# Keeping the second parts of w2 in DRAM, splitting the scores of all heads, and decoding weights in three Vector pieces

## The chip, the cores and the metric

The kernel runs on one core of a Trainium2 chip. The metric is the time of one execution on the device in microseconds (us). Five engines work beside each other and each takes its instructions strictly in the order in which the program issues them: TensorE (PE in the profile; its weight loads stand apart as PEld), VectorE (DVE), ScalarE (ACT), GpSimd (POOL) and SyncE (SP), which here issues all DMAs.

## The reference

Causal attention with a per-token decay, over 8 batches of 8 heads, 576 tokens, head size 64; then a layer norm and an MLP with a residual over the 4608 tokens of width 512 that the heads make.

```python
scores = q @ k.T / 8                                   # per head, 576 x 576
cum    = cumsum(log(clip(f, 1e-4, 1)))                 # per head
scores = where(causal, -1e9, scores + cum[:, None] - cum[None, :])
attn   = softmax(scores)                               # with 1e-9 in the denominator
x      = attn @ v                                      # heads side by side: 4608 x 512
xn     = (x - mean(x)) / sqrt(var(x) + 1e-6) * g_ln
out    = x + relu(xn @ w_ch1) @ w_ch2                  # 512 -> 2048 -> 512
```

w_ch1 and w_ch2 arrive as float64; q, k, v, f and the result are float32.

## The kernel before, in words

**Precision.** TensorE takes float32 at a slower rate and a rounded kind, float32r, at a faster one. The kernel gets float32 accuracy from the faster kind by splitting an operand into two parts, the rounded value ("high") and what is left ("low" or second part), and adding the products of high with high, high with low, and low with high. The MLP does this for weights and activations: `w1h`, `w1l`, `w2h`, `w2l` hold all parts of both weights in SBUF. Of the 64 heads (n = 8 x batch + head) the first 16 (`NFULL`) are done with plain float32 matmuls for scores and for the output; they are called full. The others split q, k, v and the probabilities.

**Weights (`WPrep`).** There are 32 items, w1 and w2 in turn, each 128 x 512 float64 values. An item is loaded as 512 KB of raw words (`wr`, 3 buffers), scaled by ScalarE (line 160, tile `wy`), decoded from float64 to float32 by four pieces on VectorE (lines 176, 177, 180, 172), the last followed by a sum on GpSimd (line 173); a w1 item also gets a column sum on TensorE (`colsum`, line 191) and four pieces that centre it (`centre`, line 199). Then ScalarE writes the high part (line 215) and GpSimd the second part (line 219). One call of `tick` moves this pipeline on by one item; the VectorE pieces go into a queue, and `fill` issues a few of them at a time. `ready()` is the number of ticks made less 5; `done()` says that all ticks (37) are made and the queue is empty.

**Slots.** The program is written as a list of 256 slots, four per head (t = 1 to 4, one tile of 128 query rows each; t = 1 also has the first 64 rows), and three slots to drain. What a slot issues, and in which order, is a string of letters; the last entry whose first slot is reached holds:

```python
ORDERS = [
    (0, "WwQsSthAeMrgFBmlLNPaRf"),
    (37, "WwQSstAMhPelgLNFrfmBRa"),
    (66, "AthQFlMSPNreamLRB"),
]
...
            elif c == "W":
                due = 1 + min(u, W_CHANGE) / W_SLOTS + max(0, u - W_CHANGE) * W_TICKS
                while not wp.done() and wp.tick_no <= due:
                    wp.tick()
```

Q: score matmuls of slot u (lines 357 to 360). S: mask, row maximum and move to SBUF on VectorE (383). e: exponential with row sum on ScalarE (394). B: reciprocal of the sum on VectorE (399, 400) and scaling on GpSimd (401). t, h, l: two slots later (`LAG`) the probabilities are transposed on TensorE (407), copied by ScalarE (457), and, for heads that are not full, their second parts made by VectorE (462). A: three slots later the output matmuls (470 or 492), for two tiles together. F, a: the output goes to `xs` (523, or 526 and 537) and for two heads together to DRAM. P: `prep`, which loads and splits the next heads (lines 329 to 344). w, g, f: `fill` with 1, 2 or 3 pieces. s: column sums. W: ticks, as above, u being the slot.

**The MLP (`Moe`)** works on chunks of 256 tokens, 18 in all, each in 16 steps j over 128 columns of the hidden layer. A step is `mm1` (12 matmuls, lines 569 to 571), a Relu and its second part (577, 582), and, one slot later, `mm2` (6 matmuls, lines 591 to 593). Letters M, r, m are the step's first half, N is `second()`, which does `mm2` of the step before, R is `rest()`, which loads and splits the next chunk's input. A slot issues its step only if `moe.can(wp.ready())` was true at its start and u is 35 or more. `can` asks that the weights of step j are there (ready at least 2(j + 1)) and that the chunk's input is. Steps left after the slots run in a loop of their own behind them.

At head 14, t = 1 (slot 56), `prep` makes all ticks that are left, closes the pool of the weight pipeline's tiles and opens the pool `late`, which holds the tiles of the split heads.

Of the kernel before, what the change touches and what calls it, by code (L numbers as in the profile page):

```python
# [11 lines left out]
I32 = mybir.dt.int32  # L12
U16 = mybir.dt.uint16
AF = mybir.ActivationFunctionType
# [4 lines left out]
P = 128  # L19
# [17 lines left out]
W_ASIDE = 6  # L37
FILL = {"f": 3, "g": 2, "w": 1}
# [17 lines left out]
def attn_moe(ctx: ExitStack, tc: tile.TileContext, qk, v, f, g, w1, w2, out):  # L56
# [6 lines left out]

    early = ExitStack()
    wpool = early.enter_context(tc.tile_pool(name="early", bufs=1))
    pools = {}

# [42 lines left out]
    def gates(h0):  # L110
        nc.vector.tensor_scalar(out=fa, in0=fa, scalar1=1e-4, scalar2=1.0, op0=ALU.max, op1=ALU.min)
        nc.scalar.activation(fb, fa, AF.Ln)
        nc.vector.tensor_tensor_scan(out=fc, data0=fones, data1=fb, initial=0.0, op0=ALU.mult, op1=ALU.add)
        nc.scalar.activation(cumr[:, 0, :], fc, AF.Copy, scale=-1.0 / SCALE)
        nc.vector.scalar_tensor_tensor(
            out=cumr[:, 1, :], in0=fc, scalar=-1.0 / SCALE, in1=cumr[:, 0, :].bitcast(F32), op0=ALU.mult, op1=ALU.subtract
        )
        nc.sync.dma_start(out=h0.kl[64:66, :], in_=cumr[0:1].bitcast(F32))
        nc.sync.dma_start(out=cumd, in_=cumr.bitcast(F32))
# [12 lines left out]
    class WPrep:  # L132
# [8 lines left out]
        def load(self, n):  # L141
# [7 lines left out]
            else:  # L149
                nc.sync.dma_start(out=raw, in_=w2.bitcast(U32)[j * P : (j + 1) * P, :])  # L150
            self.d[n] = {"raw": raw, "hw": raw.rearrange("p (n t) -> p n t", t=2)[:, :, 1]}

# [9 lines left out]
        def decode(self, n):  # L162
            layer, j = self.items[n]
            d = self.d[n]
            y, z = d["y"], d["hw"]
            low = d["raw"].bitcast(U16).rearrange("p (n t) -> p n t", t=4)[:, :, 1]
            zf, yf = z.bitcast(F32), y.bitcast(F32)
            d["w"] = yf
            ve = nc.vector

            def last():
                ve.scalar_tensor_tensor(out=zf, in0=low, scalar=2.0**-36, in1=zf, op0=ALU.mult, op1=ALU.mult)
                nc.gpsimd.tensor_tensor(out=yf, in0=yf, in1=zf, op=ALU.add)

            return [
                lambda: ve.tensor_scalar(out=z, in0=z, scalar1=0x80000000, scalar2=None, op0=ALU.bitwise_and),  # L176
                lambda: ve.scalar_tensor_tensor(  # L177
                    out=y, in0=y, scalar=3, in1=z, op0=ALU.logical_shift_left, op1=ALU.bitwise_or
                ),
                lambda: ve.tensor_scalar(out=z, in0=y, scalar1=0xFF800000, scalar2=None, op0=ALU.bitwise_and),  # L180
                last,
            ]
# [22 lines left out]
        def parts(self, n):  # L205
            layer, j = self.items[n]
            w = self.d[n]["w"]
            if layer == 1:
                fs = slice(j * P, j * P + P)
                return w.rearrange("p (k f) -> p k f", k=KT), w1h[:, :, fs], w1l[:, :, fs]  # L210
            return w, w2h[:, j, :], w2l[:, j, :]

        def high(self, n):
            w, hi, lo = self.parts(n)
            nc.scalar.copy(out=hi, in_=w)

        def low(self, n):
            w, hi, lo = self.parts(n)
            nc.gpsimd.tensor_tensor(out=lo, in0=w, in1=hi.bitcast(F32), op=ALU.subtract)
            del self.d[n]  # L220

        def tick(self):
# [19 lines left out]
            if on(t - 2 - cl, 1):  # L242
                self.high(t - 2 - cl)
            if on(t - 3, 2):
                self.low(t - 3)
# [21 lines left out]
        def done(self):  # L267
            return self.tick_no >= len(self.items) + 3 + W_SUMS and not self.queue

# [19 lines left out]

    xqs, xfs = [], []  # L290

    def new_xq(name, dt):
        xq = work.tile([66, S], dt, tag="xq", bufs=2, name=name)
        nc.gpsimd.memset(xq[64:66, :].bitcast(F32), 1.0)
        return xq

    def load(n):
        h = Head()
        h.n, h.full = n, n < NFULL
        if h.full:  # L300
            h.kl = work.tile([66, S], F32, tag="kl", bufs=2, name=f"kl{n}")
            if len(xfs) < 2:
                xfs.append(new_xq(f"xf{n}", F32))
            h.xq = xfs[n % 2]
            nc.sync.dma_start(out=h.xq[0:64, :], in_=qk[n][0:64, 0, :])
            nc.sync.dma_start(out=h.kl[0:64, :], in_=qk[n][0:64, 1, :])
            if n > 0:
                nc.sync.dma_start(out=h.kl[64:66, :], in_=cumd[n])
        else:
            h.raw = pools["late"].tile([P, 2, S], F32, tag="raw", bufs=1, name=f"raw{n}")  # L310
            nc.sync.dma_start(out=h.raw, in_=qk[n])
        return h
# [8 lines left out]
    def prep_a(h):  # L321
        n = h.n
        h.hi = pools["late"].tile([P, 2, S], F32R, tag="hi", bufs=2, name=f"hi{n}")
        h.kl = work.tile([66, S], F32R, tag="kl", bufs=2, name=f"kl{n}")
        if len(xqs) < 2:
            xqs.append(new_xq(f"xq{len(xqs)}", F32R))
        h.xq = xqs[(n - NFULL) % 2]
        nc.sync.dma_start(out=h.kl[64:66, :].bitcast(F32), in_=cumd[n])
        nc.scalar.copy(out=h.hi[:, 1, :], in_=h.raw[:, 1, :])
# [4 lines left out]
    def prep_b(h):  # L334
        nc.scalar.copy(out=h.hi[:, 0, :], in_=h.raw[:, 0, :])  # L335
        nc.vector.tensor_copy(out=h.xq[0:64, :], in_=h.raw[0:64, 0, :])
        nc.gpsimd.tensor_tensor(  # L337
# [10 lines left out]
    def qk_mm(h, t):  # L348
# [4 lines left out]
        for i, (a, z) in enumerate(cuts):  # L353
            sp = bank(f"s{h.n}_{t}_{i}")[:m, : z - a]
            xq, kl = h.xq[:, q0 : q0 + m], h.kl[:, a:z]
            if h.full:
                mm(sp, xq, kl, start=True, stop=True)  # L357
            else:
                mm(sp, h.hi[:, 0, q0 : q0 + m], h.hi[:, 1, a:z], start=True, stop=False)  # L359
                mm(sp, xq, kl, start=False, stop=True)  # L360
            h.s[t].append((a, z, sp))
# [51 lines left out]
    def transpose_unit(h, t):  # L413
# [3 lines left out]
        if t <= 2:  # L417
            if t == 1:
                h.ph1 = work.tile([P, 704], F32 if h.full else F32R, tag="ph1", bufs=1, name=f"ph1_{n}")
                h.pl1 = None if h.full else pools["late"].tile([P, 384], F32R, tag="pl1", bufs=1, name=f"pl1_{n}")  # L420
            ph = h.ph1
# [14 lines left out]
        else:  # L436
            if t == 3:
                h.ph2 = work.tile([P, 9 * P], F32 if h.full else F32R, tag="ph2", bufs=1, name=f"ph2_{n}")
                h.pl2 = None if h.full else pools["late"].tile([P, 7 * P], F32R, tag="pl2", bufs=1, name=f"pl2_{n}")
            c = 0 if t == 3 else P  # L440
# [72 lines left out]
    def finish(h):  # L513
# [10 lines left out]
        else:  # L524
            tmp = pools["late"].tile([P, S1], F32, tag="ot", bufs=1, name=f"ot{h.n}_{c0}")
            nc.scalar.copy(out=tmp[js, :w], in_=po[64:128, :w])
# [58 lines left out]

    def mm2(c, j, h):
        if j == 0:
            c.acc = [ps.tile([P, DM], F32, tag=f"acc{i}", bufs=1, name=f"acc{c.n}_{i}") for i in range(2)]
        for i in range(2):
            ts_ = slice(P * i, P * i + P)  # L590
            mm(c.acc[i], h[:, 0, ts_], w2h[:, j, :], start=(j == 0), stop=False)  # L591
            mm(c.acc[i], h[:, 0, ts_], w2l[:, j, :], start=False, stop=False)  # L592
            mm(c.acc[i], h[:, 1, ts_], w2h[:, j, :], start=False, stop=(j == FT - 1))  # L593
# [60 lines left out]
    class Moe:  # L654
# [3 lines left out]
        def fetch(self):  # L658
# [75 lines left out]
    load_v(hd[0])  # L734
    consts()
    gates(hd[0])
    wp.tick()
    for u, slot in enumerate(slots):
# [12 lines left out]
        def piece(c):  # L751
# [53 lines left out]
        def prep():  # L805

            if slot is not None:
                if t == 1 and n + 1 < NFULL:
                    start_head(n + 1)
# [11 lines left out]
                if t == 3 and n + 2 >= NFULL and n + 2 < B * H:  # L821
                    start_head(n + 2)
# [8 lines left out]
    while moe.left() > 0 or moe.prev is not None:  # L831
# [5 lines left out]
        moe.second()  # L837
        moe.rest()


# [36 lines left out]
```

## Time and profile before

| what | value |
|---|---|
| median of 3 runs | 1269.73 us |
| lowest and highest of them | 1265.62, 1269.95 us |
| profiled execution, its own time | 1260.39 us |
| span of its profile (first to last instruction) | 1258.6 us |
| mean granted TensorE clock | 0.992 |
| moved by DMA | 100.42 MB, mean 80 GB/s |

The page of the profile gives busy time by engine, the span in 40 slices, the chain of work that ended last, and the costliest groups of instructions by line of the program. A group's row reads: line, engine, operation, tile written and tiles read, shapes, count; then busy time in us and the mean length of one in ns; then the engine's idle time just before it and what ended it. A row of windows reads: stretch, its length, then busy time and number of instructions of each engine in the order PE, PEld, DVE, ACT, POOL (only the engines that the chosen lines use), granted clock, DMA share and GB/s.

### The profile page before, as it was taken

What the parts mean: (1) busy time and instruction counts of PE and PEld (TensorE: products, weight loads), DVE (VectorE), ACT (ScalarE), POOL (GpSimd) and SP (SyncE); (2) the same over time, 40 slices, a digit from 0 to 9 for tenths busy, and PEclk for the clock granted to TensorE, in tenths of its full rate; (3) what the DMA queues carried; (4) which work ended last, traced back from release to release, by engine and by line L of the source; (5) the groups of instructions that cost most, each with busy time, mean ns of one, the idle gap of its engine ahead of it and who ended that gap; (6) DMA issues with size and microseconds to landing.
All of it is one profiled execution on the core that took longest, in us unless ns stands there. A gap on an engine that the chain in (4) does not pass through costs nothing.

```text
span 1258.6 us, 24937 instructions
## 1 busy us (share of the span) xinstructions
PE 1232.6 (98%) x8148; PEld 1082.0 (86%) x8148; DVE 844.8 (67%) x2948; ACT 639.1 (51%) x1904; POOL 454.9 (36%) x545
## 2 busy tenths in 40 slices
PE   7999998999999999999999999999999999999998
PEld 5666766789999999999999999999998999999997
DVE  5879999358686868686868777777767773233232
ACT  4776555455555555555656565555555552112111
POOL 4666666243333433334344433333434330000000
PEclk8999989999999999999999999999999999999999
DMA  5444452122322232222222222323232201110100
GB/s 154 130 128 140 134 144 74 64 72 72 92 76 89 79 92 76 79 89 76 79 80 78 69 79 74 92 75 93 76 92 75 87 33 44 44 41 17 51 26 26
DMA packets 91250, 100.42 MB, mean 80 GB/s; under 512 B 26864, under 2 KB 76016, under 8 KB 91120
## 3 DMA queue, kind: packets, MB, share of 16 engines
q1 hardware_dynamic: 91120, 98.82, 25.5%
q8 instruction: 65, 1.06, 0.3%
q14 instruction: 65, 0.53, 0.1%
HBM read 79.61 MB, written 19.17 MB: 78 GB/s over the span
## 4 chain that ended last, share of the span: by engine, by line
PE 86%; DVE 10%; issue 1%; POOL 1%; ACT 1%; DMA 1%; SPq 0%; DVEq 0%; POOLq 0%; ACTq 0%
PE h L570 11%; PE h L569 10%; PE h L571 10%; PE acc L591 10%; PE acc L592 10%; PE acc L593 10%; PE tr L407 7%; PE o L492 5%; PE s L359 3%; PE s L360 3%; PE o L470 3%; DVE wy L177 2%; PE s L357 2%; DVE wr L176 1%; DVE wr L180 1%
## 5 line engine op out<-in xcount | busy, mean ns | idle before, releaser
L401 POOL TENSOR_SCALAR p<-p,st 64x64 f32<-64x64 f32 (+4 forms) x320 | 179.0, 564 | 428.1 <-DVE st L400 146.3
L570 PE MATMUL h<-x,w1h 128*128 128x256 f32 x1152 | 326.6, 283 | 3.0 <-DVE x L554 3.0
L569 PE MATMUL h<-x,w1h 128*128 128x256 f32 x1152 | 329.1, 286 | 0.0
L571 PE MATMUL h<-x,w1l 128*128 128x256 f32 x1152 | 325.2, 282 | 0.0
L577 ACT ACTIVATE hh<-h 128x256 fp32r<-128x256 f32 x288 | 110.5, 384 | 295.6 <-PE h L571 294.6
L591 PE MATMUL acc<-w2h,hh 128*128 128x512 f32 x576 | 228.3, 396 | 0.0
L592 PE MATMUL acc<-w2l,hh 128*128 128x512 f32 x576 | 227.5, 395 | 0.0
L570 PEld LDWEIGHTS h<-x,w1h 128*128 128x128 f32 x1152 | 219.5, 191 | 7.8 <-DVE x L554 3.6
L582 DVE SCALAR_TENSOR_TENSOR hh<-h,hh 128x256 fp32r<-128x256 f32 x288 | 120.8, 420 | 156.2 <-ACT hh L577 151.1
L593 PE MATMUL acc<-w2h,hh 128*128 128x512 f32 x576 | 224.8, 390 | 0.0
L394 ACT ACTIVATE p<-p,st 64x64 f32<-64x64 f32 (+4 forms) x320 | 178.5, 559 | 90.3 <-DVE st L383 89.0
L569 PEld LDWEIGHTS h<-x,w1h 128*128 128x128 f32 x1152 | 219.1, 190 | 5.0 <-issue 1.2
L571 PEld LDWEIGHTS h<-x,w1l 128*128 128x128 f32 x1152 | 219.2, 190 | 0.0
L457 ACT CAST ph<-tr 64x128 fp32r<-64x128 f32 (+4 forms) x384 | 108.9, 332 | 118.9 <-PE tr L407 108.2
L407 PE MATMUL tr<-identr,p 128*128 128x128 f32 (+1 forms) x896 | 142.6, 275 | 7.2 <-POOL p L401 6.6
L383 DVE CUSTOM_DVE_ANT_0 p<-s,mask 64x64 f32<-64x64 f32 (+4 forms) x320 | 129.9, 419 | 9.2 <-POOL p L369 3.3
L407 PEld LDWEIGHTS tr<-identr,p 128*128 128x128 f32 (+1 forms) x896 | 100.8, 131 | 38.3 <-POOL p L401 14.7
L593 PEld LDWEIGHTS acc<-w2h,hh 128*128 128x128 f32 x576 | 108.3, 188 | 24.9
L462 DVE TENSOR_TENSOR ph<-tr,ph 64x192 fp32r<-64x192 f32 x192 | 57.8, 301 | 95.6 <-ACT ph L457 91.9
L591 PEld LDWEIGHTS acc<-w2h,hh 128*128 128x128 f32 x576 | 109.2, 190 | 14.6 <-issue 0.9
L592 PEld LDWEIGHTS acc<-w2l,hh 128*128 128x128 f32 x576 | 109.3, 190 | 11.8
L337 POOL TENSOR_TENSOR hi<-raw,hi 64x576 fp32r<-64x576 f32 x48 | 73.4, 1530 | 69.0 <-ACT hi L335 64.6
(84 smaller groups left out, 1956.7 us busy)
## 6 DMA issues: line engine op xcount, KB each, us to landing
raw<-in_qk_dram SPq DMA_DIRECT2D x48, 576.0 KB
wr<-in_w_dram SPq DMA_DIRECT2D x32, 512.0 KB
vr<-in_v_dram SPq DMA_DIRECT2D x64, 160.0 KB
out_dram<-xt SPq DMA_DIRECT2D x36, 256.0 KB
xa<-xs SPq DMA_DIRECT2D x32, 160.0 KB
xb<-xs SPq DMA_DIRECT2D x32, 128.0 KB
xw<-xa SPq DMA_DIRECT2D x64, 64.0 KB
xw<-xb SPq DMA_DIRECT2D x48, 64.0 KB
```

The source lines that it names most:

```text
L383: nc.vector.tensor_tensor_reduce(out=pt[:m, a:z], in0=sp, in1=mask[:m, off + a : off + z], scale=-SCALE, scalar=3.0e38 if i == 0 else st[: ...
L394: nc.scalar.activation(pt[:m, :w], pt[:m, :w], AF.Exp, bias=st[:m, i : i + 1], scale=-1.0, accum_out=st[:m, 2:3])
L401: nc.gpsimd.tensor_scalar(out=pt[:m, :w], in0=pt[:m, :w], scalar1=st[:m, 3:4], scalar2=1.0, op0=ALU.mult, op1=ALU.mult)
L407: nc.tensor.transpose(out_, in_, ident[:m, :m])
L569: mm(ph, w1h[:, k, fs], c.x[k][:, 0, :], start=(k == 0), stop=False)
L570: mm(ph, w1h[:, k, fs], c.x[k][:, 1, :], start=False, stop=False)
L571: mm(ph, w1l[:, k, fs], c.x[k][:, 0, :], start=False, stop=(k == KT - 1))
L577: nc.scalar.activation(h[:, 0, :], c.ph, AF.Relu)
L582: nc.vector.scalar_tensor_tensor(out=h[:, 1, :], in0=ph, scalar=0.0, in1=h[:, 0, :].bitcast(F32), op0=ALU.max, op1=ALU.subtract)
L591: mm(c.acc[i], h[:, 0, ts_], w2h[:, j, :], start=(j == 0), stop=False)
L592: mm(c.acc[i], h[:, 0, ts_], w2l[:, j, :], start=False, stop=False)
L593: mm(c.acc[i], h[:, 1, ts_], w2h[:, j, :], start=False, stop=(j == FT - 1))
```

## The change

- The tile `w2l` is gone. The second part of a w2 item goes to a tile `wl` (2 buffers), and `keep`, one tick later, stores it to one of 16 DRAM tiles `w2d` (256 KB each). `done()` asks for one tick more.
- `fetch_low`, called at R and in the loop behind the slots, orders the second part for each coming step from DRAM into `w2s` (3 buffers, `W2_LOW`). `can` also asks that one such part is ordered (two, if a step still waits for its `mm2`), and `mm2` takes it from there.
- All heads load `raw`, make high and second parts, and form the scores from two matmuls; `NFULL` now only holds for the probabilities and the output. `xq` is filled by a DMA from `hi` instead of a cast on VectorE.
- The decode has three VectorE pieces and no sum on GpSimd.
- The pools are all open from the start; the forced ticks at head 14 are gone. `W_SLOTS`, `W_CHANGE` and `W_ASIDE` have other values. `ORDERS` is the same.

```diff
-W_SLOTS, W_CHANGE, W_TICKS = 2.82, 37, 1.1
+W2_LOW = 3
+W2_WAIT = 2
+ALL = 2 * NCHUNK * FT + W2_WAIT
+W_SLOTS, W_CHANGE, W_TICKS = 1.85, 68, 1.1
-W_ASIDE = 6
+W_ASIDE = 5
...
-    w2l = const.tile([P, FT, DM], F32R, tag="w2l", name="w2l")
+    w2d = [dram.tile([P, DM], F32, tag=f"w2d{j}", name=f"w2d{j}") for j in range(FT)]
...
-                lambda: ve.tensor_scalar(out=z, in0=y, scalar1=0xFF800000, scalar2=None, op0=ALU.bitwise_and),
-                last,
+                lambda: ve.scalar_tensor_tensor(
+                    out=y, in0=low, scalar=29, in1=y, op0=ALU.logical_shift_right, op1=ALU.bitwise_or
+                ),
...
-            return w, w2h[:, j, :], w2l[:, j, :]
+            return w, w2h[:, j, :], wpool.tile([P, DM], F32R, tag="wl", bufs=2, name=f"wl{j}")
...
+        def keep(self, n):
+            layer, j = self.items[n]
+            if layer == 2:
+                nc.sync.dma_start(out=w2d[j], in_=self.d[n]["lo"].bitcast(F32))
             del self.d[n]
...
-            if t >= n + 3 + cl:
+            if t >= n + 4 + cl:
                 return
...
         def done(self):
-            return self.tick_no >= len(self.items) + 3 + W_SUMS and not self.queue
+            return self.tick_no >= len(self.items) + 4 + W_SUMS and not self.queue
...
-        nc.vector.tensor_copy(out=h.xq[0:64, :], in_=h.raw[0:64, 0, :])
+        nc.sync.dma_start(out=h.xq[0:64, :].bitcast(F32), in_=h.hi[0:64, 0, :].bitcast(F32))
...
-            if h.full:
-                mm(sp, xq, kl, start=True, stop=True)
-            else:
-                mm(sp, h.hi[:, 0, q0 : q0 + m], h.hi[:, 1, a:z], start=True, stop=False)
-                mm(sp, xq, kl, start=False, stop=True)
+            mm(sp, h.hi[:, 0, q0 : q0 + m], h.hi[:, 1, a:z], start=True, stop=False)
+            mm(sp, xq, kl, start=False, stop=True)
...
+        low = []
+        low_no = 0
+
+        def fetch_low(self, weights):
+
+            while len(self.low) < W2_LOW and self.low_no < NCHUNK * FT and weights >= 2 * (self.low_no + 1) + W2_WAIT:
+                j = self.low_no % FT
+                self.low.append(work.tile([P, DM], F32R, tag="w2s", bufs=W2_LOW, name=f"w2s{self.low_no}"))
+                nc.sync.dma_start(out=self.low[-1].bitcast(F32), in_=w2d[j])
+                self.low_no += 1
+
         def can(self, weights):
 
+            if len(self.low) < (1 if self.prev is None else 2):
+                return False
...
-                mm2(c, j, h)
+                mm2(c, j, h, self.low.pop(0))
...
+    prep_a(hd[0])
+    prep_b(hd[0])
+    start_head(1)
     gates(hd[0])
...
                 moe.rest()
+                moe.fetch_low(ALL if wp.done() else wp.ready())
...
-                if n == NFULL - 2 and t == 1:
-                    while not wp.done():
-                        wp.tick()
-                        wp.fill(99)
-                    early.close()
-                    pools["late"] = ctx.enter_context(tc.tile_pool(name="late", bufs=1))
-                if n + 1 >= NFULL and n + 1 < B * H:
+                if n + 1 < B * H:
...
         moe.rest()
+        moe.fetch_low(ALL)
```

More of the change, by code (lines that the diff above doesn't have):

```diff
@@ L12 @@
 I32 = mybir.dt.int32
-U16 = mybir.dt.uint16
 AF = mybir.ActivationFunctionType
@@ L164, in decode @@
             d = self.d[n]
[L165 to L168, printed above, removed]
+            y, z, low = d["y"], d["hw"], d["lw"]
+            d["w"] = y.bitcast(F32)
             ve = nc.vector
-            def last():
-                ve.scalar_tensor_tensor(out=zf, in0=low, scalar=2.0**-36, in1=zf, op0=ALU.mult, op1=ALU.mult)
-                nc.gpsimd.tensor_tensor(out=yf, in0=yf, in1=zf, op=ALU.add)
             return [
@@ L210, in parts @@
                 return w.rearrange("p (k f) -> p k f", k=KT), w1h[:, :, fs], w1l[:, :, fs]
-            return w, w2h[:, j, :], w2l[:, j, :]
+            return w, w2h[:, j, :], wpool.tile([P, DM], F32R, tag="wl", bufs=2, name=f"wl{j}")
         def high(self, n):
-            w, hi, lo = self.parts(n)
-            nc.scalar.copy(out=hi, in_=w)
+            d = self.d[n]
+            d["w"], d["hi"], d["lo"] = self.parts(n)
+            nc.scalar.copy(out=d["hi"], in_=d["w"])
         def low(self, n):
-            w, hi, lo = self.parts(n)
-            nc.gpsimd.tensor_tensor(out=lo, in0=w, in1=hi.bitcast(F32), op=ALU.subtract)
+            d = self.d[n]
+            nc.gpsimd.tensor_tensor(out=d["lo"], in0=d["w"], in1=d["hi"].bitcast(F32), op=ALU.subtract)
+        def keep(self, n):
+            layer, j = self.items[n]
+            if layer == 2:
+                nc.sync.dma_start(out=w2d[j], in_=self.d[n]["lo"].bitcast(F32))
             del self.d[n]
@@ L243, in tick @@
                 self.high(t - 2 - cl)
+            if on(t - 4, 2):
+                self.keep(t - 4)
+            if on(t - 4 - cl, 1):
+                self.keep(t - 4 - cl)
             if on(t - 3, 2):
@@ L288, in attn_moe @@
         pass
[L290 to L295, printed above, removed]
+    xqs = []
     def load(n):
@@ L299, in load @@
         h.n, h.full = n, n < NFULL
-        if h.full:
[L301 to L308, printed above, removed]
-        else:
-            h.raw = pools["late"].tile([P, 2, S], F32, tag="raw", bufs=1, name=f"raw{n}")
-            nc.sync.dma_start(out=h.raw, in_=qk[n])
+        h.raw = late.tile([P, 2, S], F32, tag="raw", bufs=1, name=f"raw{n}")
+        nc.sync.dma_start(out=h.raw, in_=qk[n])
         return h
@@ L322, in prep_a @@
         n = h.n
-        h.hi = pools["late"].tile([P, 2, S], F32R, tag="hi", bufs=2, name=f"hi{n}")
+        h.hi = late.tile([P, 2, S], F32R, tag="hi", bufs=2, name=f"hi{n}")
         h.kl = work.tile([66, S], F32R, tag="kl", bufs=2, name=f"kl{n}")
         if len(xqs) < 2:
-            xqs.append(new_xq(f"xq{len(xqs)}", F32R))
-        h.xq = xqs[(n - NFULL) % 2]
-        nc.sync.dma_start(out=h.kl[64:66, :].bitcast(F32), in_=cumd[n])
+            xqs.append(work.tile([66, S], F32R, tag="xq", bufs=2, name=f"xq{n}"))
+            nc.gpsimd.memset(xqs[n][64:66, :].bitcast(F32), 1.0)
+        h.xq = xqs[n % 2]
+        if n > 0:
+            nc.sync.dma_start(out=h.kl[64:66, :].bitcast(F32), in_=cumd[n])
         nc.scalar.copy(out=h.hi[:, 1, :], in_=h.raw[:, 1, :])
@@ L419, in transpose_unit @@
                 h.ph1 = work.tile([P, 704], F32 if h.full else F32R, tag="ph1", bufs=1, name=f"ph1_{n}")
-                h.pl1 = None if h.full else pools["late"].tile([P, 384], F32R, tag="pl1", bufs=1, name=f"pl1_{n}")
+                h.pl1 = None if h.full else late.tile([P, 384], F32R, tag="pl1", bufs=1, name=f"pl1_{n}")
             ph = h.ph1
@@ L438, in transpose_unit @@
                 h.ph2 = work.tile([P, 9 * P], F32 if h.full else F32R, tag="ph2", bufs=1, name=f"ph2_{n}")
-                h.pl2 = None if h.full else pools["late"].tile([P, 7 * P], F32R, tag="pl2", bufs=1, name=f"pl2_{n}")
+                h.pl2 = None if h.full else late.tile([P, 7 * P], F32R, tag="pl2", bufs=1, name=f"pl2_{n}")
             c = 0 if t == 3 else P
@@ L524, in finish @@
         else:
-            tmp = pools["late"].tile([P, S1], F32, tag="ot", bufs=1, name=f"ot{h.n}_{c0}")
+            tmp = late.tile([P, S1], F32, tag="ot", bufs=1, name=f"ot{h.n}_{c0}")
             nc.scalar.copy(out=tmp[js, :w], in_=po[64:128, :w])
@@ L591, in mm2 @@
             mm(c.acc[i], h[:, 0, ts_], w2h[:, j, :], start=(j == 0), stop=False)
-            mm(c.acc[i], h[:, 0, ts_], w2l[:, j, :], start=False, stop=False)
+            mm(c.acc[i], h[:, 0, ts_], low, start=False, stop=False)
             mm(c.acc[i], h[:, 1, ts_], w2h[:, j, :], start=False, stop=(j == FT - 1))
@@ L820, in prep @@
                         prep_b(hd[n + 1])
-                if t == 3 and n + 2 >= NFULL and n + 2 < B * H:
+                if t == 3 and n + 2 < B * H:
                     start_head(n + 2)
```

16 lines of the change are left out of this document (6 added, 10 removed).

## The prediction

> **What bounds the kernel now.** I read the page first, then stages by windows, then single lines within a stage, then the timeline where a row had to be dated.
>
> ```profile
> span 1258.6 us, 24937 instructions
> PE 1232.6 (98%) x8148; PEld 1082.0 (86%) x8148; DVE 844.8 (67%) x2948; ACT 639.1 (51%) x1904; POOL 454.9 (36%) x545
> PE 86%; DVE 10%; issue 1%; POOL 1%; ACT 1%; DMA 1%; SPq 0%; DVEq 0%; POOLq 0%; ACTq 0%
> ```
>
> TensorE is busy for 98% of the span and is 86% of the chain that ended last. What keeps it full is the interleaving: an MLP step (18 matmuls) is laid between the attention work of each slot. The Relu copy of line 577 occurs once per step, so its counts date the steps; the softmax exponential of line 394 leaves two records for each of five tiles per head, so ten records are four slots.
>
> ```profile
> 106.00:263.00 157.00, 8.79 (x24) 0.97 0.33 100
> 263.00:1034.30 771.30, 72.94 (x190) 1.00 0.26 80
> 1034.30:1258.60 224.30, 28.80 (x75) 1.00 0.12 35
> 1053.30:1252.20 198.90, 26.49 (x70) 1.00 0.11 32
> ```
>
> ```profile
> 13.30:105.80 92.50, 27.33 (x88) 0.94 0.44 133
> 105.80:263.00 157.20, 24.58 (x78) 0.97 0.33 100
> ```
>
> In the first fence (line 577 alone) 24 steps lie in 106 to 263 us, 190 in 263 to 1034 us, one in each of the 190 slots left, and 75 run after the last slot. The fourth row begins and ends at such a copy: 69 steps in 198.9 us, 2.88 us a step with TensorE full. In the second fence (line 394 alone) 88 records are 35 slots in 92.5 us, 2.64 us a slot, and 78 are 31 slots (35 to 65). A slot with its step takes 771.3/190 = 4.06 us: the step's 2.88 us and only 1.2 us for the attention beside it. That is the whole merit of the order: attention's long waits between engines are covered by steps.
>
> **The change, part by part. First the gate,** because it decides everything else. A step runs in a slot only if `can` says so. It now also wants a streamed second part of w2, and `fetch_low` orders number m (from 1) only when ready >= 2m + 2, until `done()` lifts the bound. ready is the tick counter less 5. `done()` now wants 38 ticks (32 items + 4 + 2). Ticks are made by the letter W alone, while the counter is not above 1 + u/1.85 in slot u. The diff removes the loop that forced the remaining ticks at head 14, and leaves ORDERS alone: from slot 66 on the order is "AthQFlMSPNreamLRB", which has no W. In slot 65 the bound is 1 + 65/1.85 = 36.1, so the counter goes from 36 to 37, and stops there, one tick short. ready stays at 32, so m stops at 15, and `done()` is never true while slots last. Fifteen steps use up the fifteen parts; then `can` is false in all slots from 67 to 255. Only the loop behind the slots calls `fetch_low` without a bound. The same counting for the kernel before gives 24 steps through slot 66, which is the x24 above. So in place of 24 + 190 + 75 steps (one on the border) there are 15 in the first 67 slots, none in the next 189, and 273 after the last slot.
>
> **Slots 66 to 255, 190 of them, now attention alone.** What does such a slot take? Four stages follow each other through two engines that work strictly in order: the transposed copies on ScalarE (line 457), their second parts on VectorE (462), the score reduction on VectorE (383), the exponential on ScalarE (394), behind which the next slot's copies stand in ScalarE's queue. The rows of 300 to 1000 us, each for one line, in the order 394, 383, 457, 462:
>
> ```profile
> 300.00:1000.00 700.00, 135.56 (x430) 1.00 0.26 81
> ...
> 300.00:1000.00 700.00, 111.12 (x516) 1.00 0.26 81
> ...
> 300.00:1000.00 700.00, 104.51 (x387) 1.00 0.26 81
> ...
> 300.00:1000.00 700.00, 138.38 (x386) 1.00 0.26 81
> ```
>
> 430 records are 43 heads: 3.15 + 2.58 + 2.43 + 3.22 = 11.4 us a head, 2.85 us a slot, if nothing overlaps and no hop costs anything. A third copy and a first exponential overlap a little; each hop adds some hundredth to a tenth. The rest of both engines fits into the other's turns: VectorE's row sums and reciprocals (lines 399 and 400) and the output sums (537):
>
> ```profile
> 300.00:1000.00 700.00, 29.43 (x214) 1.00 0.26 81
> ...
> 300.00:1000.00 700.00, 34.72 (x214) 1.00 0.26 81
> ...
> 300.00:1000.00 700.00, 38.35 (x86) 1.00 0.26 81
> ```
>
> Lower bound: VectorE alone, (111.12 + 138.38 + 29.43 + 34.72 + 38.35)/43 = 8.2 us a head, 2.05 us a slot, if the ring came apart. Upper bound: today's whole slot, 4.06 us, as a step can only add. I take 3.05 us, the serial ring and 0.2 us for hops and late matmuls: 190 x 3.05 = 580 us, where 771 us held 190 steps as well.
>
> **The steps behind the slots.** 273 x 2.88 = 786 us. The cover to test is the stream: one DMA of 256 KB a step, 288 in all, SP's queue in order, three buffers. The DMA for step i+3 waits for the second matmuls of step i and is due two steps and the first matmuls later, 2 x 2.88 + 1.4 = 7.1 us. Queued behind that wait on SP stand the chunk's input loads and stores; they are now released once a step, and their readers come two steps later. How long does a load take?
>
> ```profile
> 2.64 0.59 SPq L145 DMA_DIRECT2D wr<-in_w_dram  x1
> 3.27 0.51 SPq L150 DMA_DIRECT2D wr<-in_w_dram  x1
> ...
> 8.58 0.68 ACT L160 ACTIVATE wy<-wr 128x512 f32<-128x512 f32 x1 [0.61 <-DMA wr<-in_w_dram]
> ```
>
> The second 512 KB load, behind some 1.1 MB, was there 5.3 us after its issue; half the bytes on queues busy for 11% fit into 7.1 us. I cost the stream at nothing; uncovered, by these rows it is at most 5.3 - 2.88 = 2.4 us a step. The 16 stores (`keep`) go beside idle queues.
>
> **Slots 0 to 65.** Weight preparation goes at 0.54 items a slot instead of 0.36 and then 1.1, and every head now gets its second parts.
>
> ```profile
> L329 ACT CAST hi<-raw 128x576 fp32r<-128x576 f32 x48 | 32.6, 679 | 0.0
> L335 ACT CAST hi<-raw 128x576 fp32r<-128x576 f32 x48 | 32.3, 673 | 0.6
> L173 POOL TENSOR_TENSOR wy<-wy,wr 128x512 f32<-128x512 f32 x32 | 42.2, 1318 | 26.5 <-issue 16.0 <-DVE wr L172 6.2 <-POOL p L401 1.6
> L177 DVE SCALAR_TENSOR_TENSOR wy<-wy,wr 128x512 uint32<-128x512 uint32 x32 | 38.6, 1205 | 0.0
> L172 DVE SCALAR_TENSOR_TENSOR wr<-wr 128x512 f32<-128x512 uint16 x32 | 22.5, 705 | 0.3
> L180 DVE TENSOR_SCALAR wr<-wy 128x512 uint32<-128x512 uint32 x32 | 22.2, 693 | 0.6
> L336 DVE CAST xq<-raw 64x576 fp32r<-64x576 f32 x48 | 50.6, 1055 | 0.0
> ```
>
> - Decoding: lines 172 and 180 go (1.40 us an item on VectorE), one piece like 177 comes, 0.7 (like 172) to 1.2 us; GpSimd's 1.32 us go. VectorE gains 0.2 to 0.7 us an item.
> - Head preparation for 16 more heads: 0.68 + 0.67 us on ScalarE, 0.34 us a slot; GpSimd gets two subtractions a head for the sums it lost.
> - The 48 casts of line 336 become a DMA each behind ScalarE's copy; its reader comes a slot later, so it costs nothing, and VectorE's 50.6 us are off the ring (it ran beside the exponential), so they bring nothing.
> - Start: 576 KB for head 0, two casts and one more DMA ahead of the gates' rows on SP: 3 us (0 to 5).
>
> Slots 0 to 34: before 2.64 us; ScalarE gets 0.34 us and 0.18 more items (0.2 us), VectorE a little: 2.64 (all hidden) to 3.25, taken 3.05. 13.3 + 3 + 35 x 3.05 = 123 us.
>
> ```profile
> 115.00:215.00 100.00, 91.52 (x514) 70.36 (x515) 96.99 (x240) 52.30 (x144) 66.27 (x58) 0.95 0.40 119
> 215.00:263.00 48.00, 48.00 (x284) 37.50 (x283) 18.39 (x78) 22.74 (x74) 15.64 (x22) 1.00 0.16 53
> ```
>
> Columns: TensorE, its loads, VectorE, ScalarE, GpSimd. In 115 to 215 us VectorE was full (97.0 of 100) with an item in every slot; that jam goes. In 215 to 263 us ten slots with a step each and no items took 4.75 us. Now slots 35 to 65 hold 15 steps and 16 slots without: 15 x 4.75 + 16 x 3.1 = 121 us. Slot 66 begins at 244 us (230 to 262), against 263 us.
>
> Scores: four float32 matmuls of 288 columns against two pairs of the split kind:
>
> ```profile
> 139.22 1.13 PE L357 MATMUL s<-kl,xf 66*128 66x288 f32 x4
> 607.09 0.38 PE L359 MATMUL s<-hi 128*128 128x288 f32 x1
> 607.57 0.30 PE L360 MATMUL s<-kl,xq 66*128 66x288 f32 x1
> ```
>
> 1.13 us against 607.09 to 607.87, 0.78 us: a third less, some 1 us a head; these slots do not wait for TensorE, and I count none of it.
>
> **Sum.** 244 + 580 + 5 (three draining slots) + 786 + 5 (last copy to end of span) = 1620 us of span. The profiled execution took 1260.39 us for a span of 1258.6 us, and the median of the three runs is 1269.73 us, 9 us above it. So 1630 us for the median.
>
> **Rivals.**
> 1. *The clock falls in slots 66 to 255.* Three windows of the start, TensorE count first, granted clock third from the end:
>
> ```profile
> 20.00:27.00 7.00, 6.34 (x29) 3.41 (x26) 3.32 (x14) 3.96 (x14) 2.79 (x5) 0.93 0.45 144
> 27.00:34.00 7.00, 6.70 (x26) 3.71 (x26) 4.64 (x19) 4.27 (x14) 1.74 (x3) 0.76 0.16 53
> 157.00:164.00 7.00, 5.24 (x17) 3.49 (x18) 6.97 (x14) 1.66 (x4) 5.30 (x5) 0.54 0.37 117
> ```
>
> With 29, 26 and 17 matmuls in 7 us the clock was 0.93, 0.76 and 0.54. An attention slot has 10 matmuls, 23 in 7 us at 3.05 us, and lies between. At half clock the output matmuls push the transposes, and with them the copies, late: with 10 matmuls a slot at twice their time, I estimate 3.5 us, so 190 x 0.45 = 85 us more, 1715 us. Against it: the ring leaves TensorE over a microsecond of slack a slot. The Trainium skill ("TensorE: Matmul & The Clock Gate", Part 1) says the clock falls to half after an idle window of about 3.4 us, and its Part 4 that transposes do not count as busy in the same way; 14 of 40 matmuls a head are transposes, so by that rule this case is the likelier one. The three rows agree with the first sentence.
>
> 2. *The stream bounds the steps.* If SP's waits made a step 3.3 us, 273 x 0.42 = 115 us more: 1745 us. For it: everything passes SP in order; against it: 4 us of slack.
>
> 3. *The gate opens after all* (a tick I do not see), one step a slot from slot 70. Then slot 66 at 244 us with 9 steps fewer, 26 us: 7 us later than now, 1277 us. This is also the case that can end faster: it does if slot 66 comes before 263 - 26 = 237 us, that is if VectorE, freed of the jam of 115 to 215 us, runs slots 0 to 34 at 2.64 us; then 230 us, 1263 us, and with the rest of the score matmuls' 16 us some 1250 us. The count of 24, which the same reading gives, speaks against a missed tick.
>
> **How the numbers follow.** Forecast 72%, clock 14%, stream 9%, open gate 5% (2 faster, 1 same, 2 slower). Within the forecast the ring may be 2.75 to 3.25 us (-57 to +38 us) and slot 66 at 230 to 262 us (-14 to +18 us). The range, 1565 to 1720 us, takes in the clock; the stream and the open gate stay out. 0.5% (6 us) is what a measurement can tell here.
>
> **What would show it.** Line 577's count: 15 before slot 66, none until some 825 us, 273 after. In between TensorE's busy share falls, ScalarE and VectorE wait for each other on lines 457, 462, 383 and 394, and each slot takes about 3 us. The last 785 us have TensorE full and a step each 2.88 us. The prediction is wrong if steps run between 300 and 800 us; mis-sized if slots take 3.5 us at a clock under 0.8, or if `acc` waits for the streamed tile.

## The result, and the profile after

The changed kernel takes 1655.6 us (median of 4 runs, 1651.8 to 1659.7). The kernel before took 1267.7 us on the same chip (4 runs). The ratio is 1.306, 95% interval [1.3015, 1.3107]. The forecast was 1630 us with a range of 1565 to 1720. The profiled execution took 1654.12 us for a span of 1652.3 us; my sum was 1620 us of span. Ratios here and below leave out slow executions, of which there was one: one of the four of run 9 took 4158.1 us, for a reason that no trace shows.

From the page of the changed kernel: span, busy time by engine, TensorE's busy share and its granted clock in 40 slices of 41 us each, the chain that ended last, and the streamed matmuls.

```profile
span 1652.3 us, 25757 instructions
PE 1422.9 (86%) x8148; PEld 1238.2 (75%) x8148; DVE 799.5 (48%) x2868; ACT 669.3 (41%) x1937; POOL 447.8 (27%) x543
PE   5878987767777777776679999999999999999999
PEclk7778998666666666666669999999999999999999
PE 69%; ACT 9%; issue 9%; DVE 5%; POOL 5%; DMA 2%; POOLq 0%; SPq 0%; ACTq 0%; DVEq 0%
L583 PE MATMUL acc<-w2s,hh 128*128 128x512 f32 x576 | 226.8, 394 | 5.5 <-DMA w2s<-w2d 5.5
```

TensorE runs the same 8148 matmuls as before, now in three stages that the slices show: some 290 us mixed, 570 us at 0.7 busy with the clock at 0.6, then 790 us full. Its share of the chain fell from 86% to 69%. The last row says that the second matmuls of the MLP waited 5.5 us for the stream in the whole run.

The Relu copy (line 568 here, 577 before) dates the steps: window, its length, busy time and count of that line, clock, DMA share and GB/s.

```profile
20.10:146.80 126.70, 0.00 (x0) 0.76 0.54 171
146.80:271.50 124.70, 5.56 (x15) 0.96 0.54 164
271.50:858.20 586.70, 0.07 (x1) 0.64 0.28 84
867.00:1652.30 785.30, 104.88 (x273) 1.00 0.43 126
```

Fifteen steps have started when slot 66 begins, none starts in slots 67 to 255 (the one record of 0.07 us in the third row is the end of the fifteenth copy), and 273 run behind the slots, where the kernel before had 75. The gate is shut, as counted. Slots 66 to 254 take (858.2 - 271.5)/189 = 3.10 us each.

Now the first row. I had slot 0 at 16 us and slot 35 at 123 us. They begin at 20.1 and 146.8 us (the start of the slot's exponential over 128 rows, here and below), so 35 slots take 126.7 us: 3.62 us a slot, where the kernel before has 2.64 and I had taken 3.05. All engines in the same stages (TensorE, its weight loads, VectorE, ScalarE, GpSimd, clock):

```profile
20.00:147.00 127.00, 96.55 (x429) 68.17 (x427) 89.97 (x284) 80.71 (x233) 75.96 (x80) 0.76 0.54 171
271.50:858.00 586.50, 416.50 (x1943) 358.49 (x1943) 386.42 (x1606) 354.47 (x1084) 296.02 (x377) 0.64 0.28 84
```

No engine is full in the first 127 us: TensorE 76%, VectorE 71%, ScalarE 64%, GpSimd 60%. Somebody waits. The waits of that stage (waiting line, releaser, us in total, times, longest):

```profile
PEld s L350 <- POOL hi L331: 27.2, 8, 5.1
PE s L350 <- POOL hi L331: 25.3, 8, 4.8
PE s L351 <- DMA xq<-hi: 1.6, 3, 0.8
```

Eight head boundaries lie in it, and TensorE waits at them for the second part of the new head's q (line 331 on GpSimd). Its busy time (96.55 us) and its two waits (25.3 and 1.6 us) make up all but 4 us of the stage. One boundary in the timeline (start, duration, engine, line; in brackets the wait):

```profile
71.18 0.67 ACT L329 CAST hi<-raw 128x576 fp32r<-128x576 f32 x1
71.88 0.47 SPq L330 DMA_DIRECT2D xq<-hi  x1
72.10 1.40 POOL L331 TENSOR_TENSOR hi<-raw,hi 64x576 fp32r<-64x576 f32 x1
73.56 0.24 PE L350 MATMUL s<-hi 128*64 128x64 f32 x1 [1.62 <-POOL hi L331]
74.33 0.21 PE L351 MATMUL s<-kl,xq 66*64 66x64 f32 x1 [0.53 <-DMA xq<-hi]
```

Cast, subtraction and scores follow each other: a cast of 0.67 us, the subtraction of 1.40 us 0.25 us later, and the first score matmul 0.06 us after that. The preparation is issued at t = 3, with one slot between it and its reader, behind that slot's other work in ScalarE's and GpSimd's queues, and arrives when it is needed or later.

### The profile page after: what moved, and what is told of

Same layout as the page of the kernel before. It is cut to its first block, busy times and chain, and to the rows that moved or that the text cites. A ratio compares the mean times of both kernels' runs of the same rounds, so it can differ in the third digit from the quotient of the medians.

```text
span 1652.3 us, 25757 instructions
## 1 busy us (share of the span) xinstructions
PE 1422.9 (86%) x8148; PEld 1238.2 (75%) x8148; DVE 799.5 (48%) x2868; ACT 669.3 (41%) x1937; POOL 447.8 (27%) x543
## 4 chain that ended last, share of the span: by engine, by line
PE 69%; ACT 9%; issue 9%; DVE 5%; POOL 5%; DMA 2%; POOLq 0%; SPq 0%; ACTq 0%; DVEq 0%
PE o L483 9%; PE h L560 8%; PE h L562 8%; PE h L561 8%; PE acc L583 8%; PE acc L582 8%; PE acc L584 8%; PE tr L398 5%; ACT ph L448 5%; ACT p L385 3%; PE o L461 3%; POOL vv L338 2%; POOL hi L331 2%; DVE p L374 1%; DVE ph L453 1%
## 5 line engine op out<-in xcount | busy, mean ns | idle before, releaser
L392 POOL TENSOR_SCALAR p<-p,st 64x64 f32<-64x64 f32 (+4 forms) x320 | 175.6, 551 | 297.7 <-DVE st L390 103.6
L398 PE MATMUL tr<-identr,p 128*128 128x128 f32 (+1 forms) x896 | 210.2, 372 | 34.2 <-POOL p L392 33.6
L583 PE MATMUL acc<-w2s,hh 128*128 128x512 f32 x576 | 226.8, 394 | 5.5 <-DMA w2s<-w2d 5.5
L483 PE MATMUL o<-ph,vv 128*128 128x256 f32 (+2 forms) x384 | 101.8, 412 | 138.7 <-POOL vv L338 106.8
L483 PEld LDWEIGHTS o<-ph,vv 128*128 128x128 f32 x384 | 84.5, 298 | 170.0 <-POOL vv L338 121.2
L350 PE MATMUL s<-hi 128*128 128x288 f32 (+4 forms) x384 | 172.6, 466 | 39.0 <-POOL hi L331 36.9
L398 PEld LDWEIGHTS tr<-identr,p 128*128 128x128 f32 (+1 forms) x896 | 140.0, 178 | 65.5 <-POOL p L392 52.8
L351 PE MATMUL s<-kl,xq 66*128 66x288 f32 (+4 forms) x384 | 142.0, 374 | 4.8 <-DMA kl<-cumr 3.2
L350 PEld LDWEIGHTS s<-hi 128*128 128x128 f32 (+1 forms) x384 | 100.3, 262 | 47.4 <-POOL hi L331 39.6
```

The lines of the kernel that those rows point to most:

```text
L392: nc.gpsimd.tensor_scalar(out=pt[:m, :w], in0=pt[:m, :w], scalar1=st[:m, 3:4], scalar2=1.0, op0=ALU.mult, op1=ALU.mult)
L398: nc.tensor.transpose(out_, in_, ident[:m, :m])
L483: mm(o, st, mv, start=first, stop=True, skip_group_check=True)
L583: mm(c.acc[i], h[:, 0, ts_], low, start=False, stop=False)
```

## The experiments

Two questions: is the shut gate the whole of the loss, and what made the first 35 slots longer than I had them? "Slot n at" is the start of its exponential over 128 rows.

**1. Ticks also from slot 66 on** (changed kernel, gate opened).

```
-    (66, "AthQFlMSPNreamLRB"),
+    (66, "WAthQFlMSPNreamLRB"),
```

> The changed kernel with one letter more: the order from slot 66 on begins with W, so that the tick that was missing is made in slot 67. Theory 1 (the gate): the lost time was steps shut out of the slots by that one tick. Then 15 steps through slot 67, one in each slot after it, 85 behind the slots; slot 66 at 271 us as now, 188 slots of 4.06 us, 85 x 2.88 = 245 us: about 1295 us of span, 1.02 times the kernel before. Theory 2 (the stream): steps with their second part from DRAM are too slow beside attention, whatever the gate; then the time stays above 1400 us and TensorE waits for the streamed tile.

Measured: 1297.8 us, ratio to before 1.029 [1.026, 1.032]. The Relu copy:

```profile
0.00:283.90 283.90, 5.63 (x15) 0.83 0.53 161
283.90:1045.30 761.40, 72.28 (x188) 1.00 0.51 155
1045.30:1298.00 252.70, 32.63 (x85) 1.00 0.42 121
```

One letter brings one step into every slot from 67 on and takes 358 us off. Slot 66 came at 280.8 us here, 9 us later than in the changed kernel with the same instructions up to there, so differences of some us in the first slots between two runs say little. The gate is the cause; the change still costs 3%.

**2. The kernel before with its steps stopped at 15** until the slots end: the gate's effect with nothing else of the change.

```
-        want = moe.can(wp.ready()) and u >= FIRST_MOE
+        want = moe.can(wp.ready()) and u >= FIRST_MOE and moe.left() > NCHUNK * FT - 15
```

> The kernel before with the gate shut by hand: after 15 steps no step is issued in a slot, the other 273 run behind the slots; nothing else of the change. Theory 1 (the gate alone): 15 steps are made by slot 57, at 218 us; 198 slots of 3.1 us and 273 x 2.88 us follow: about 1625 us, all but some 30 us of the loss. Theory 2 (streaming, or the split scores): the steps behind the slots need no DMA here, so clearly less, under 1500 us.

Measured: 1658.5 us (one run). Without the stream, the split scores of the first 16 heads or the new decoding, the loss is as large. What it added is in its attention-only slots:

```profile
246.00:859.00 613.00, 419.14 (x1927) 361.82 (x1926) 426.48 (x1642) 353.36 (x1079) 297.73 (x374) 0.63 0.22 69
```

(859.8 - 245.8)/188 = 3.27 us a slot, 0.16 more than in the changed kernel, at the same clock and with VectorE busier (70% against 66%). Run 12 finds out why.

**3. A warmer clock in the attention-only slots:** the changed kernel with eight matmuls of weights, whose result is overwritten, ahead of each tile's transposes from head 17 on.

```
+    def keep_warm(h, tp):
+        if h.n >= 17:
+            for _ in range(8):
+                mm(tp[:, 0:256], identr, w1h[:, 0, 0:256], start=True, stop=True, skip_group_check=True)
```

> The changed kernel, still shut, with eight matmuls of 256 columns more ahead of the transposes of every tile of heads 17 to 63, whose results the transposes overwrite; they fill TensorE's idle time. Theory A (the clock costs): the granted clock in 280 to 850 us, 0.64 now, comes to 0.95 or more and the slots shrink from 3.10 to about 2.85 us, some 45 us in all, to 1610 us. Theory B (the ring of ScalarE and VectorE sets the slot): the clock rises, but the slots stay within 0.05 us of 3.10 us and the time at 1655 us.

Measured: 1711.4 us (one run). The clock rose to 0.91, and the slots became longer, (917.6 - 296.4)/185 = 3.36 us:

```profile
288.00:917.00 629.00, 484.27 (x3411) 457.05 (x3410) 383.46 (x1596) 354.93 (x1079) 293.64 (x374) 0.91 0.26 78
```

A transpose (line 398) took 303 ns on average here and 394 ns in the changed kernel, but the fillers stand ahead of it in TensorE's queue. ScalarE's copies waited for TensorE 97.7 us in 300 to 900 us (36.4 us put down to the transposes, 61.3 us to the score matmuls beside them), 0.55 us a slot; in the changed kernel it is 0.30 us a slot, as shown further below. That difference of 0.25 us is the whole difference of the slots. Neither theory fits: late transposes are a part of what a slot takes, and fillers make them later. What a higher clock alone would bring, this run does not separate.

**4. The old rate of ticks** in the changed kernel, which opens the gate by slot 66 too, as the ticks come early enough.

```
-W_SLOTS, W_CHANGE, W_TICKS = 1.85, 68, 1.1
+W_SLOTS, W_CHANGE, W_TICKS = 2.82, 37, 1.1
```

> The changed kernel with the old rate of ticks (2.82 and 37 in place of 1.85 and 68), all else as changed. All 38 ticks are made by slot 59. Theory 1 (the gate): steps run in every slot from then on, 24 by slot 66 as before; the first 35 slots keep the cost of the heads' preparation (slot 35 at 125 to 140 us against 106), the next are no slower than before: 1275 to 1290 us. Theory 2 (the stream): above 1400 us.

Measured: 1284.5 us, ratio 1.017 [1.014, 1.020]; slot 35 at 139.0 us, slot 66 at 288.3 us with 23 steps done. The gate again, from its other side. Slot 35 is still 33 us later than before (105.8 us), with fewer items than in the changed kernel, so decoding was not the main load there.

**5. Head preparation one slot earlier,** added to run 4.

```
-                    if t == 2:
+                    if t == 1:
                         prep_a(hd[n + 1])
-                    if t == 3:
+                    if t == 2:
                         prep_b(hd[n + 1])
-                if t == 3 and n + 2 < B * H:
+                if t == 2 and n + 2 < B * H:
```

> Differs from the run with the old rate of ticks (2.82, 37: 1284.5 us, slot 35 at 139.0 us against about 123 before) in one thing: prep_a runs at t = 1, prep_b at t = 2 and the next load at t = 2, one slot earlier each. Theory 'second part of q comes too late at the head boundary' (TensorE waited 25.3 us for the POOL subtraction in eight head boundaries of 20-147 us): slot 35 falls to 120-128 us and the time to 1262-1275 us. Theory 'the clock of 0.76 and the decoding set these slots': slot 35 stays at 135-142 us and the time at 1278-1290 us.

Measured: 1259.7 us, ratio 0.9973 [0.9958, 0.9988], 24.8 us less than run 4. Slot 35 at 119.5 us. Waits of 20 to 147 us in run 4 (first fence) and here (second), then 20 to 110 us of run 4 and of this run with all engines:

```profile
PE s L350 <- POOL hi L331: 17.3, 8, 3.5
```

```profile
PE s L350 <- POOL hi L331: 3.1, 5, 1.0
```

```profile
20.00:110.00 90.00, 73.09 (x311) 48.44 (x309) 55.07 (x192) 56.52 (x168) 48.67 (x56) 0.73 0.47 144
```

```profile
20.00:110.00 90.00, 78.31 (x383) 50.62 (x383) 63.72 (x233) 67.79 (x205) 60.77 (x67) 0.85 0.58 180
```

The wait shrinks by 14 us, and 383 matmuls instead of 311 fit into the same 90 us. The clock went from 0.73 to 0.85 with nothing done to it but the earlier preparation. The result lies just beyond the range of the first theory (slot 35 at 120 us or later, 1262 us or more) and far from the rival (clock and decoding set these slots: slot 35 at 135 us or later). So the late preparation is shown as the cause; how much of the 25 us is the wait itself, and how much the clock that rose with it, is not separated.

**6. The stream alone,** in the kernel before: `keep`, `fetch_low`, the tile `low` in `mm2` and the new condition in `can`, heads and decoding as before.

```
-            mm(c.acc[i], h[:, 0, ts_], w2l[:, j, :], start=False, stop=False)
+            mm(c.acc[i], h[:, 0, ts_], low, start=False, stop=False)
```

> The kernel before with one part of the change: second parts of w2 written to DRAM and read back for each step, ticks, heads and decoding as before (all ticks are forced at slot 56, so the gate opens). Theory 'the stream is free' (256 KB a step took 5.5 us issue to landing, three in flight, a step takes 2.88 us at best): 1260-1275 us. Rival 'the stream costs each step or each slot': from 1290 us up, spread over the slots from 35 on and the steps behind them.

Measured: 1263.5 us, ratio 1.0006 [0.9990, 1.0023]. The stream is free.

**7. The three-piece decoding alone,** in the kernel before.

```
-                lambda: ve.tensor_scalar(out=z, in0=y, scalar1=0xFF800000, scalar2=None, op0=ALU.bitwise_and),
-                last,
+                lambda: ve.scalar_tensor_tensor(
+                    out=y, in0=low, scalar=29, in1=y, op0=ALU.logical_shift_right, op1=ALU.bitwise_or
+                ),
```

> The kernel before with the other part alone: weights decoded in three VectorE pieces, without the fourth piece and GpSimd's addition. Theory 'VectorE and GpSimd set the first 56 slots': the 32 items save about 0.5 us each on VectorE, 1245-1262 us. Rival 'TensorE or ScalarE sets them': 1262-1270 us.

Measured: 1245.3 us, ratio 0.9864 [0.9832, 0.9895]: faster than both kernels. The window in which VectorE was full before (97.0 of 100 us), and its two long pieces:

```profile
115.00:215.00 100.00, 100.00 (x592) 77.50 (x591) 76.81 (x244) 59.90 (x172) 42.59 (x46) 1.00 0.42 128
```

```profile
L172 DVE SCALAR_TENSOR_TENSOR wy<-wy,wr 128x512 uint32<-128x512 uint32 x32 | 32.3, 1009 | 0.0
L175 DVE SCALAR_TENSOR_TENSOR wy<-wr,wy 128x512 uint32<-128x512 uint32 x32 | 26.7, 836 | 0.6
```

VectorE falls to 77 us, TensorE rises from 91.5 to 100 us: in this stage the bound passes from VectorE to TensorE. Slots 35 to 65 take 143.0 us instead of 157.4.

**8. xq by a transfer alone,** in the kernel before.

```
-        nc.vector.tensor_copy(out=h.xq[0:64, :], in_=h.raw[0:64, 0, :])
+        nc.sync.dma_start(out=h.xq[0:64, :].bitcast(F32), in_=h.hi[0:64, 0, :].bitcast(F32))
```

> The kernel before with one line of the head preparation changed: xq of the heads from 16 on copied by a transfer from hi and not by VectorE from raw. My prediction held this to be worth nothing; the kernel before with its steps stopped had attention-only slots of 3.27 us against 3.10 us in the changed kernel, so 0.16 us a slot may be due to it. If it counts in full slots too, 192 slots by 0.16 us: 1235-1245 us; if TensorE covers it there: 1258-1270 us; if the transfer comes late at the head boundary: above 1272 us.

Measured: 1262.7 us, ratio 0.9994 [0.9970, 1.0018]. Nothing, with a step in each slot.

**9. Both repairs of the changed kernel,** runs 1 and 5 together, at the change's own rate of ticks.

> The changed kernel with two repairs: ticks also run from slot 66 on (W put into the third entry of ORDERS, 1297.8 us by itself), and the head preparation one slot earlier. If the late second part of q cost the first 35 slots 25 us here as with the old rate of ticks: 1268-1278 us. If the later ticks of this rate hold the steps back as well and the two overlap: 1285-1298 us.

Measured: 1280.4 us, ratio 1.012 [1.009, 1.016], between the two expectations. Against run 1 the earlier preparation brings 17 us here, against 25 us at the old rate; the first 35 slots take 110.7 us here and 130.9 us in run 1. Against run 5 the rate costs 20.7 us. Through slot 66 this run has 15 steps done, run 5 has 23, and behind the slots it has 85 against 76. Nine steps more behind the slots are 9 x 2.88 = 26 us, and its slots end 7 us sooner (1025.9 against 1033.1 us). The slower ramp of ticks after slot 37 holds the steps back; that it prepares more items earlier does not pay.

**10. Decoding and stream together,** the change without its heads (edits of 6 and 7 in the kernel before).

> The kernel before with the three-piece decoding and the streamed second parts, that is, the whole change without the heads (scores of the first 16 heads stay in float32, old rate of ticks). If the two parts add: 1242-1252 us, and what the run with everything and the early preparation (1259.7 us) has above it, 10 to 17 us, belongs to the scores of the first 16 heads. If the stream takes the gain of the decoding: 1255-1263 us.

Measured: 1243.7 us, ratio 0.9852 [0.9805, 0.9900]. The parts add. Run 5 lies 16 us above. It has besides the split scores of the first 16 heads with their preparation, the transfer of xq (nothing by run 8) and no forced ticks at slot 56; these were not run apart. Its slot 0 begins at 20.5 us, in run 10 at 11.8 us (8.7 us later), the first 35 slots take 99.1 against 96.9 us, slots 35 to 65 take 144.6 against 139.9 us.

**11. Decoding with the ticks somewhat faster** (2.3 in place of 2.82 in run 7).

> The kernel before with the three-piece decoding and the ticks at one in 2.3 slots and not 2.82 up to slot 37, so that fewer items are left for slots 37-56. If VectorE's items still set slots 35-66 with the shorter decoding: 1232-1242 us. If TensorE sets them (busy 125.00 of 125.00 us in 147-272 us of the three-piece run): 1242-1250 us.

Measured: 1244.1 us, ratio 0.9855 [0.9821, 0.9889], no different from run 7. TensorE sets these slots once the decoding is shorter.

**12. Run 2 with xq by a transfer** (edits of 2 and 8).

> The kernel before with its steps stopped at 15 until the slots end (attention-only slots of 3.27 us, 1658.5 us) and xq copied by a transfer from hi in place of VectorE's cast. If the cast, 1.07 us a head on VectorE, is part of the ring in slots without a step: slots of 3.08 to 3.13 us as in the changed kernel, 26 to 36 us less, 1622 to 1633 us. If the 0.16 us a slot belong to something else of the change: slots of 3.24 to 3.30 us, 1650 to 1665 us.

Measured: 1628.7 us (one run), slots of (830.4 - 248.0)/188 = 3.10 us. The cast of 1.07 us a head is worth 0.17 us a slot where no step covers it, and nothing (run 8) where one does.

The ladder, each rung against the one above it. The rungs were measured on four occasions; the kernel before had medians of 1262.4 to 1262.6 us on those of runs 1 to 11 and 1267.7 us beside the changed kernel, so the last rung is uncertain by some 5 us. The rung of -2 us is within the noise.

| kernel | us | difference |
|---|---|---|
| before (beside runs 5 to 8) | 1262.5 | |
| three-piece decoding (7) | 1245.3 | -17 |
| and the stream (10) | 1243.7 | -2 |
| and the heads as changed (split scores in all), prepared early (5) | 1259.7 | +16 |
| and prepared one slot later, as in the change (4) | 1284.5 | +25 |
| and the change's rate of ticks, gate open (1) | 1297.8 | +13 |
| and the gate shut (the changed kernel) | 1655.6 | +358 |

## Why the prediction was right, and where it missed

**The gate: right.** Fifteen steps through slot 66, none until the slots end, 273 behind. Runs 1, 2 and 4 show it from three sides: one letter, or another rate, opens it; and shut in the kernel before, it costs 396 us there (1658.5 against 1262.4). The rival in which it opens had no part in it.

**Attention-only slots: right, 3.10 us against 3.05.** The ring of four stages, in the order exponential, score reduction, transposed copies, their second parts:

```profile
300.00:850.00 550.00, 140.04 (x444) 0.63 0.28 85
300.00:850.00 550.00, 114.25 (x532) 0.63 0.28 85
300.00:850.00 550.00, 107.97 (x401) 0.63 0.28 85
300.00:850.00 550.00, 143.08 (x398) 0.63 0.28 85
```

550/3.10 = 177 slots, and (140.04 + 114.25 + 107.97 + 143.08)/177 = 2.85 us a slot, as worked out; 0.25 us are left where I had 0.2 for hops and late matmuls. The waits of 300 to 850 us follow the ring: ScalarE for the score reduction, VectorE for the transposed copies, and ScalarE's copies for TensorE (the last two rows).

```profile
ACT p L385 <- DVE st L374: 157.5, 177, 1.9
DVE ph L453 <- ACT ph L448: 85.3, 154, 1.1
PE o L483 <- POOL vv L338: 102.1, 44, 2.8
ACT ph L448 <- PE tr L398: 42.3, 44, 1.0
ACT ph L448 <- PE s L350: 11.0, 28, 0.5
```

TensorE's own longest waits are the output matmuls, once a head, for v's second part on GpSimd (third row). Little of that reaches the copies. The other group of output matmuls of a head does hold them up, once a head (fourth row). One such place:

```profile
564.44 1.33 PE L483 MATMUL o<-ph,vv 128*128 128x256 f32 x5 [0.30 <-DVE ph L453]
565.56 0.95 PE L483 MATMUL o<-pl,vv 128*64 128x256 f32 x4
566.31 0.67 PE L398 MATMUL tr<-identr,p 128*64 128x128 f32 x3
567.07 0.47 ACT L448 CAST ph<-tr 64x192 fp32r<-64x192 f32 x2 [0.81 <-PE tr L398]
567.58 0.35 DVE L453 TENSOR_TENSOR ph<-tr,ph 64x192 fp32r<-64x192 f32 x1 [0.93 <-ACT ph L448]
```

Nine output matmuls stand for 2.07 us ahead of the transposes, ScalarE waits for these, and VectorE for ScalarE. The two last rows of the waits are (42.3 + 11.0)/177 = 0.30 us a slot. Without them the slot is 2.80 us, and run 3 gives the same, 3.36 - 0.55 = 2.81 us. So what the slot takes above the ring is late transposes; what the hops between the stages add is made up for by overlap. That my 0.2 us came near this was partly luck: I had named late matmuls in that term, but worked out no size for them.

**"They bring nothing" for the casts of line 336: wrong in these slots, right elsewhere.** Run 12 gives 0.17 us a slot for them. I had taken the cast to run beside the exponential. The forecast of 3.05 us came out all the same, since it was worked out from rows without the cast.

**Steps behind the slots: right.** 273 in 785 us, with the end of the span; the forecast had 786 + 5. The stream costs nothing: 5.5 us of waits in all, and run 6.

**Clock, the first rival: half right.** The clock did fall, to 0.64. The rule in the Trainium skill ("TensorE: Matmul & The Clock Gate", Part 1) that the clock falls to half after an idle window of about 3.4 us points the same way, but no row here bears it out: TensorE's longest wait in 300 to 850 us was 2.8 us. In the three rows that I said agree with it, TensorE's longest idle time was 3.1 us, up to 158.8 us. The way in which I let the rival act, output matmuls that push the transposes and with them the copies, is there, but not at the price of 0.45 us a slot: all waits of the copies for TensorE are 0.30 us a slot. A part of these is the clock: the nine output matmuls took 2.07 us, and 1.22 us in run 3 at a clock of 0.91, so I estimate at most (2.07 - 1.22)/4 = 0.2 us a slot. My argument against the rival, over a microsecond of slack a slot on TensorE, was wrong as an argument, since the output matmuls come in a bunch just ahead of the transposes. Run 3 shows that warming the clock by fillers costs more than the low clock.

**The first 35 slots: the term that was mis-sized.** Of the 32 us that the span came out longer than the sum, 27.5 lie ahead of slot 66: 3.8 us at the start, 20 us in slots 0 to 34, 3.7 us in slots 35 to 65. The rest is 10 us in the slots with no step and 5 us less behind them. The step that failed is the one on head preparation: I counted its instructions as load on ScalarE and GpSimd, and looked at the arrival of the transfer of xq alone, of which I wrote that its reader comes a slot later, so that it costs nothing. I had not followed cast and subtraction through their queues to the time of arrival. TensorE waited 25.3 us for that subtraction. Moved one slot earlier at the change's own rate of ticks (run 9), the first 35 slots take 110.7 us, 3.16 us a slot and close to the 3.05 I had taken, against 126.7 us in the changed kernel and 130.9 us in run 1: 16 to 20 us. The start was also outside its bound (0 to 5 us): slot 0 began 6.8 us later than before, and run 5 against run 10 gives 8.7 us.

**Decoding: right in kind, the worth too small.** Per item VectorE gained 0.705 + 1.205 + 0.693 - 1.009 - 0.836 = 0.76 us in run 7, just over my 0.2 to 0.7. I let the jam of 115 to 215 us go, which run 7 confirms; alone the edit is worth 1.4%, and the rest of the change hides it.

**Median against profile:** I added 10 us to the span for the median; it lies 3 us above. That took back a part of the error in the span.

## What to carry to other kernels

When a condition is tightened, follow every counter in it to its last value: here a loop bounded by a rate stopped one tick short of a test that one letter in an order had to reach, and 358 us hung on it. Work moved ahead of a reader must be costed by its arrival, through each queue that it passes, and not by its busy time alone. An engine's slack on average does not cover work that comes in a bunch ahead of what others wait for: nine matmuls in a row held up two engines here, with TensorE idle for 29% of the stage. Time the parts of a bundled change one by one: one part of this one (the decoding) was worth 1.4% by itself, and the other parts with the shut gate turned that into a loss of 31%.

## What the runs showed of the hardware

A VectorE instruction with two operands in SBUF can be stretched when GpSimd runs beside it. In run 7 two pieces of decoding of the same kind and shapes, 10 us apart, with GpSimd's rows of the same time:

```profile
61.86 1.65 DVE L175 SCALAR_TENSOR_TENSOR wy<-wr,wy 128x512 uint32<-128x512 uint32 x1
71.07 0.68 DVE L172 SCALAR_TENSOR_TENSOR wy<-wy,wr 128x512 uint32<-128x512 uint32 x1
```

```profile
61.26 1.71 POOL L215 TENSOR_TENSOR w2l<-wy,w2h 128x512 fp32r<-128x512 f32 x1
68.10 1.26 POOL L215 TENSOR_TENSOR w1l<-wy,w1h 128x512 fp32r<-128x512 f32 x1
```

The piece at 61.86 us overlaps GpSimd's subtraction and takes 1.65 us; the one at 71.07 us begins after GpSimd's is over and takes 0.68 us. They are two lines of the program, but line 175 too takes 0.69 us in the 21 cases with no GpSimd instruction beside it. Over the kernel before, line 177 (the same operation on the same shapes) took 0.69 us in the 6 cases with no GpSimd instruction beside it and 1.32 us on average, from 0.67 to 2.95 us, in the 26 with one. So part of the gain of run 7 may come from the GpSimd addition that it drops: line 177 fell from 1205 to 1009 ns though nothing in it changed. The Trainium skill ("SBUF — State Buffer", Who interferes with whom) states it as a lock on a shared port, which these rows agree with. With one operand both cases occur: the cast of v (line 337 of the changed kernel) took 0.481 us each time, and the cast of q (line 336 of the kernel before) took 0.45 us in the one case with no GpSimd instruction beside it and 1.07 us on average in the 47 with one.
